# Pair units in 64-row tiles, even-odd tokens up to the store, low-rank products in row tiles, and totals carried by small transfers

## The chip, the cores and the metric

The kernel runs on one NeuronCore of a Trainium2 chip. The metric is device time in microseconds (us) of that core. Times and profiles come from the chip; in the profile PE is the matrix engine (TensorE), PEld its weight loads, DVE the VectorE, ACT the ScalarE, POOL the GpSimd engine, and SP the engine whose queue issues most of the transfers.

## The reference, cut to what matters

There are two stages. The first is a gated linear recurrence for 4 batches x 8 heads, 768 tokens, head size 48; the second adds a low-rank mix along the tokens and a two-layer MLP with a ReLU.

```
for t in range(S):                       # S = 768, state is D x D per head, D = 48
    state = alpha[:, :, t, :, None] * state + einsum('bhd,bhe->bhde', k[:, :, t], v[:, :, t])
    y[:, :, t] = einsum('bhd,bhde->bhe', q[:, :, t], state)
x = y as (batch, token, head * D)        # 4 x 768 x 384
h = x.transpose(0, 2, 1) @ U @ V         # U 768 x 32, V 32 x 768: mixes the tokens
u = x + h.transpose(0, 2, 1)
out = u + maximum(u @ w_ch1, 0) @ w_ch2  # 384 -> 1536 -> 384
```

## The kernel before

**Chunks.** The recurrence is computed in chunks of 128 tokens. Within a chunk the logarithms of alpha are summed up to each token by a matrix product with a triangle of ones; their exponentials scale q (upward) and k (downward); the scores, k times q, are masked to the lower triangle; the chunk's output is masked scores times v, plus q times the state that came into the chunk; and the state for the next chunk is (old state + scaled k times v), times the total decay of the chunk. Products run on TensorE in bf16 and land in PSUM[...]; DVE, ACT and GpSimd do the rest.

**Two layouts.** Batches 2 and 3 use `stage_gla`, one chunk of 128 tokens and all 8 heads a time: six units a batch. Batches 0 and 1 (`PAIR`) use `stage_pair`, which takes 256 tokens of 4 heads: partition p holds tokens 2p and 2p + 1 of the block (index j), so each descriptor of a load carries two tokens. A unit has two chunks (index c): the lower 64 partitions are chunk 0, the upper 64 chunk 1. The heads are taken in pairs (index a).

**Tokens in the pair units.** The transposed q (`qT`) is written by a copy with a stride (`f_ev` with swap), which puts a chunk's tokens in natural order. Scores (L486) run in 64 x 64 tiles of the array, four at a time. Outputs (L560 and L567) and state products (L518) run over all 128 rows: for that v lies in a wide buffer `rw` that has zeros where the other chunk would be, filled by two casts a unit (`f_rv`), so that one product of 96 or 192 columns serves both chunks, half of it on zeros.

**The mix.** `stage_mix` multiplies x by U for six chunks (L727): each product has 32 output rows, and the four column groups of the array (128 x 32 tiles) work side by side, each on other chunks, so that PSUM holds four partial sums on 128 partitions. V is there four times (`vm_sb`, made through `sel`), so that one product over all 128 rows adds them up: six products a batch (L758), and for batch 0 (`XT`) the same into the transposed layout (L749) and once more in the second MLP product (L836). After it come transposes (L774), the first MLP product (`mlp1`, L801, 72 matmuls a batch) and the second (`mlp2`, L831), with an add (L843) and a store (L848).

**Totals.** The decay of a chunk is needed per row of the state. In `stage_gla`, four products with one column of ones (L592) put the sums of a chunk across the partitions, and two exponentials (L605) with an offset of -30000 on the half that is not wanted make `tot` of them, by which `f_st` (L687) multiplies.

**What sets the order.** Each `P.add` records one step with the engines that it may run on, what it reads and writes, and, for TensorE, the shape of the array's tiles (F full, R 64 x 128, Q 64 x 64, C 128 x 32, V for 32 rows). The string `TABLE` lists the steps by number; a letter names the engine where a step has several (A for ACT, V for DVE, G for GpSimd). `Plan.run` emits them in exactly this order, so that TABLE sets each engine's order and, with it, SP's queue of loads and stores. `Plan.place` gives out buffers and PSUM banks along the way. In the first 28 us, products of zeros (`filler`, L317) are put in where the plan has gaps.

**Loads.** 24 loads of 192 KB a batch (alpha, k, q, v for six units) and 24 of the weights go into 36 buffers `io`; a load waits in SP's queue until its buffer is free. Batch 3 transposes q and k by a transfer from ACT's queue (L623) and not on TensorE.

Of the kernel before, what the change touches and what calls it, by code (L numbers as in the profile page):

```python
# [159 lines left out]
69 65 61 201 157 179 63 64 62 160 204 162 165V 73 66 67 71 77 159A 161 164G 158G 167 182 169V 184 163 206 183 207 224 205 75 166 173 70 168V 186V 174  # L160
187V 170 227 229 175 188 209V 189 68 191A 232G 228 247 171 211 190V 176 172 192 194 234 250 78 208G 230 213A 180A 251 236A 185 210 181G 212V 195 177 81
214 254G 193 178V 3 256 268 252 253 196 215 74 271 72 79 197 76 4 231G 82 83 80 273 199 233 203A 202G 235A 84 198 258V 216 217 255G 272 218 226G 219
274 225A 237 85 93 6 257 5 259A 222 220 240 25 29 27 89 15 17 13 19 23 21 87 33 94 35 86 31 238 239 200A 275G 223A 95 90 221 241 260 276V 242 277 249G
248G 279A 278 2 270G 243 245 261 263 244 262 47 92 280A 264 91 97 37 43 269A 281 265 284 39 41 51 49 101 88 45 285 266 96 0 1 8 30G 28G 283 282 286 388
246A 432 391 435 267V 287 298 18G 11 9 16G 14G 288V 394 7A 289 105 57 59 53 55 290 438 437 436 10A 12V 102 291A 100 103 20G 295 292 304 301 98 293 294V
24G 22G 307 296 299 302 308 297V 305 26A 410 99 306V 303V 413 300A 326 322 107 309A 350 336 416 393 392 337V 310 414 396G 334 324 325A 415 311V 327V
335V 351V 323V 34G 32G 104 106 109 108 110 344 342 320 340 346 338 318 321A 36A 343V 395V 319A 314 398 330 341A 345A 315A 339V 439V 417V 400V 440G 356
354 412G 117 111 357V 355V 397 352 441 328 331A 347A 443V 419 442 316 411A 418G 353V 329V 444V 420 332 455 399A 333A 317A 426 348 312 421V 422V 40A
349A 38G 44G 42G 427 458 313V 428 423 429G 390G 46G 401 445 460 459 461 48A 52A 425 446 424 402 368 358 363 433G 434G 389G 50A 478 430 481 482 483 484
54G 60G 58A 499 369 447 431V 403 373 359 404 364 448 405 406 407V 449 450V 485V 408 502 56A 503 456A 409V 486V 365 370 451 371 487 462G 463V 488 504  # L170
457A 507G 360 471 489A 490A 505 465 467A 464 361 366 479A 480A 113 367 119 118 466V 472 374 491 473G 506G 468 492 375 509 494 453 469 470 511A 112 508
474 452G 378 495 618 475G 620 476 510A 376 501A 496G 621 454V 512 493 500G 515 624G 379 514 497 516 517G 513 626 623 657 622 625V 477A 129 362 114 115
659 518 662 498A 519A 627 380 629A 520 521A 637 660 628V 630 381 632 383 661 663G 664G 619G 522 524 133 121 523 525 530 384 536 534 528 531 529 537 535
526 385 527A 532 116 120 124 125 127 141 123 122 134 533V 126 665 131 372 137 135 639 666 668V 633 538 539V 634 640 641 540 642 562 548 558 542 541A
563V 643G 644G 572 646 549V 559V 717 648V 631 667V 573A 645 544 582 556 677 647A 545A 557A 649 832 669 130 128 386 583V 671 566 568 670 651 650 554 719
546 584 567A 543A 721 720 555V 697 658A 585V 586 679 547V 587V 569V 578 681 722 638G 834 652 574 635 653 575V 836 835 680 636A 682 837 387 153 655 560
550 580 684V 656V 654V 552 699 683G 553V 551A 867 701 838G 704G 570 686 685 564 579V 581V 571V 565V 702 700 678A 561A 672 703V 687V 724V 593 588 706
705 692 594 595 673 598 589 675 145 132 674V 693 707V 596 708V 839V 676V 840 688A 849 709 689 711 710 691 690 723G 851 599 725 727A 576 698G 726 600
590 712 854 577A 869 841 728A 852 718A 591 694V 872 870 613 614 729 713 731 730 138 149 382 377 143 136 142 885 921 853 871 714G 147 139 615 603 887
715 732 695 601 716V 696V 604 842 733A 889 734 923 608 735A 855G 874G 616 844 843 738 748 873G 833G 744 903 888 925 924 926 742 609 749 743 745 602 592  # L180
140 146 155 154 750 751 739 892G 610 736 746 605 752 737 850G 890 875 876 747V 753V 740 845 847 905 846 794 796 741V 797V 606 856G 891G 927G 778 768
774 848A 857 611 795V 894 858 908 893 906 760 780 764 862 152 150 144 761V 148 151 612 156 617 775V 781V 765V 863 769V 788 782 800 790 798 784 791V
779V 785V 772 758 759V 789A 907 799A 773A 801A 754 755V 756 757V 877 859 895 860 861 878 896 904A 783A 776 762 928G 864G 807 770 766 929 930 868G 909G
886G 910G 763V 767V 771V 911 802 865 912 880 803 916 808 897 777V 881 882G 879 809 898 804 812 883 813 899 900V 810 805 931 913 917 932 884A 866A 914
933 915 918G 786 792 901 827 811 806 922G 793A 902A 787A 822 934 919 920A 823 824 935V 936 828 937A 829 938 940 946 825 939 947 941 817 814 944 826 597
607 945 818 942 948 949V 943A 950 819 820 951 956 966 968 952 830 953 815 962 974 954 960 975V 970 963V 955V 976 982 994 969V 961V 995V 971A 967V 1000
992 988 993A 977A 957A 978 986 964 987V 1001V 980 958 989V 981V 959A 984 1002 990 996 983A 965A 1003A 985V 991V 997A 998 999A 972 1014 1024 1015 1004
1025 1026 1019 1020 1027 979V 973V 1021 1005 1009 1010 831 816 1028 1022 1006 1016 1007 1011 1023 821 1008 1017 1029 1012 1030 1032 1018 1013 1031 1033
1034
# [3 lines left out]
def mm(*cols):  # L193
    return sum(max(c / 2.4 + 2.5, 25.0) for c in cols)
# [3 lines left out]
def kernel(  # L198
# [12 lines left out]
    nc = tc.nc  # L211
# [20 lines left out]
    TRD = {(3, c) for c in range(NC)}  # L232
# [5 lines left out]
    u_in = const.tile([128, NC, R], FP32, name="u_in")  # L238
    v_in = const.tile([R, S], FP32, name="v_in")
# [9 lines left out]
    mask2 = const.tile([C, 2, 2 * C], BF16, name="mask2")  # L249
    for x in (filler, tri, ident, mask2, blocks):  # L250
# [6 lines left out]
        out=mask2, in_=mask2, compare_op=ALU.is_gt, fill=1.0, base=0, pattern=[[1, 2], [-1, 2 * C]], channel_multiplier=2  # L257
# [26 lines left out]
    nc.vector.tensor_copy(maskp[0:64, 0], mask2[0:64, :, 0:C])  # L284
    nc.vector.tensor_copy(maskp[64:128, 0], mask2[64:128, :, C : 2 * C])
    rv2_s = slots("rw", 4, [C, 2, HP, 2, D], BF16)
    for x in rv2_s:
        nc.vector.memset(x, 0.0)
    maskc = const.tile([C, 1, C], BF16, name="maskc")
    P.add({"POOL": 250}, lambda e: nc.gpsimd.tensor_copy(maskc[:, 0, :], ut_ones), w=["maskc"])  # L290
    sel = const.tile([R, 4, R], BF16, name="sel")
# [8 lines left out]
    tots = Pool(slots("tot", 4, [128, HP * 2, 1], FP32))  # L300
    qts = Pool(slots("qt", 4, [128, HP, C], BF16))
# [31 lines left out]
    def small():  # L333
        P.add({"SP": 450.0}, lambda e: nc.sync.dma_start(u_in, moe_U.rearrange("(c p) r -> p c r", p=128)), w=["u_in"])
        P.add({"SP": 500.0}, lambda e: nc.sync.dma_start(v_in, moe_V), w=["v_in"])
        P.add({"POOL": 300, "ACT": 280}, lambda e: copy(e, u_sb, u_in), r=["u_in"], w=["u"])
        P.add({"POOL": 800}, lambda e: nc.gpsimd.tensor_copy(v_bf, v_in), r=["v_in"], w=["v_bf"])
        for i in range(2):
            vb = Buf(bank)
            sl = slice(i * TW, (i + 1) * TW)  # L340
            P.add({"PE": mm(TW)}, lambda e, vb=vb, sl=sl: nc.tensor.matmul(vb()[:, 0:TW], lhsT=sel.rearrange("r a b -> r (a b)"), rhs=v_bf[:, sl], start=True, stop=True), r=["v_bf"] + [("sel", g) for g in range(4)], w=[vb], mode="V")
            P.add({"DVE": 470, "ACT": 390}, lambda e, vb=vb, sl=sl: copy(e, vm_sb[:, sl], vb()[:, 0:TW]), r=[vb], w=[("vm", i)])

    def weight(dst, src, key, engs):
        t = Buf(io)
        P.add({"SP": 590.0}, lambda e: nc.sync.dma_start(flat(t), src), w=[t])
        P.add(engs, lambda e: copy(e, dst, flat(t)), r=[t], w=[key])
# [4 lines left out]
    def weights1():  # L352
        for g in range(4):
            cs = slice(g * DM, (g + 1) * DM)
            for ct in range(NCT):
                weight(w1_sb[:, ct, cs], moe_w_ch1[ct * 128 : (ct + 1) * 128, cs], ("w1", g, ct), {"POOL": 485, "ACT": 435})

    def weights2():
        for jt in range(NJ):
            weight(w2_sb[:, jt, :], moe_w_ch2[jt * 128 : (jt + 1) * 128, :], ("w2", jt), {"POOL": 485, "ACT": 435})  # L360
# [24 lines left out]
    def xk(b, xb, c):  # L385
        return [(xb, c, 0), (xb, c, 1)] if b in PAIR else [(xb, c)]

    def stage_pair(b, u, sprev, xb):
# [12 lines left out]
        rv = Buf(rv2s)  # L401
# [5 lines left out]
        for c in range(2):  # L407
            P.add({"POOL": 480, "ACT": 420}, lambda e, c=c: f_rv(e, c), r=[vt], w=[(rv, c)])
# [494 lines left out]
```

## Time and profile before

| what | before |
|---|---|
| three runs: median (lowest to highest) | 164.61 us (163.31 to 165.84) |
| the profiled execution, in all | 164.47 us |
| its span, first to last instruction | 162.7 us |
| PE busy, share of the span | 154.3 us, 95% |
| DVE | 125.8 us, 77% |
| ACT | 85.4 us, 52% |
| POOL | 57.7 us, 35% |
| granted TensorE clock | 0.998 |
| HBM read, written | 23.79 MB, 4.72 MB |

A row of the groups gives line, engine, operation, what is written and read, shape and count; then the busy time and the mean of one; then the engine's idle time just before, and what ended it. Matmuls overlap in the array, so their mean is longer than the step from one to the next; the steps come from the starts. A row of the chain of waits has the start, the length and the work. A row of stretches has, for each, its bounds and length, the busy time of the five engines with counts, the clock, the DMA share and GB/s.

### The profile page before, as it was taken

Reading aid. Unit: us, or ns where it says so; the run is one execution under the profiler, and the core shown is the slowest. Engines: PE = TensorE matmul, PEld = TensorE weight load, DVE = VectorE, ACT = ScalarE, POOL = GpSimd, SP = SyncE. Lnnn points to the kernel's source line nnn. Section 1 sums busy time; section 2 is a strip of 40 time slices with the busy share of each in tenths; the row PEclk is TensorE's granted clock in tenths of the full one; section 3 lists DMA queues with packets and bytes.
Section 4 is the critical chain, followed back from the end, with each engine's and each line's share of the span. In section 5 each row is a group of like instructions: output and inputs, shape, how many; then the busy total and the mean of one; then the engine's idle time right before and its main releaser. Section 6 shows DMA issues by size and latency. Waiting matters only on the chain.

```text
span 162.7 us, 4458 instructions
## 1 busy us (share of the span) xinstructions
PE 154.3 (95%) x1683; PEld 102.4 (63%) x1683; DVE 125.8 (77%) x274; ACT 85.4 (52%) x218; POOL 57.7 (35%) x92
## 2 busy tenths in 40 slices
PE   7789999999999899999999999999899999999993
PEld 2356787667776676766666666766466656666662
DVE  6478996689969996979999888988978557961441
ACT  5479899557885778468982386307102411153000
POOL 3037985756264172550092056634413000000000
PEclk9999999999999999999999999999999999999999
DMA  5999999999999998998997898989982040200134
GB/s 124 271 279 302 250 277 285 326 316 330 355 253 248 207 209 185 186 202 168 216 246 64 198 204 209 218 135 189 218 108 99 0 144 7 97 0 4 48 145 145
DMA packets 89701, 30.37 MB, mean 187 GB/s; under 512 B 83376, under 2 KB 89648, under 8 KB 89680
## 3 DMA queue, kind: packets, MB, share of 16 engines
q1 hardware_dynamic: 83152, 28.52, 71.1%
q10 hardware_dynamic: 6528, 1.57, 7.4%
q8 instruction: 13, 0.21, 0.6%
q14 instruction: 8, 0.07, 0.1%
HBM read 23.79 MB, written 4.72 MB: 175 GB/s over the span
## 4 chain that ended last, share of the span: by engine, by line
PE 84%; DVE 6%; ACT 3%; DMA 3%; issue 1%; SPq 1%; DVEq 0%; ACTq 0%
PE ps L801 29%; PE ps L831 27%; PE ps L459 3%; DMA io<-in_alpha_dram 3%; PE ps L653 2%; PE ps L567 2%; PE ps L774 2%; DVE rq L446 2%; PE ps L486 2%; PE ps L758 2%; PE ps L632 2%; PE ps L518 1%; PE ps L712 1%; PE ps L590 1%; DVE st L531 1%
## 5 line engine op out<-in xcount | busy, mean ns | idle before, releaser
L831 PE MATMUL ps<-w_sb,h1t 128*128 128x384 bf16 (+2 forms) x300 | 53.1, 319 | 0.0
L801 PE MATMUL ps<-uT,w_sb 128*128 128x384 bf16 x288 | 50.9, 326 | 0.0
L801 PEld LDWEIGHTS <-w_sb 128*128 128x128 bf16 x288 | 26.8, 98 | 16.2 <-DVE uT L326 0.2
L831 PEld LDWEIGHTS <-h1t 128*128 128x128 bf16 x300 | 27.2, 98 | 15.2 <-issue 0.3
L813 DVE TENSOR_SCALAR h1t<-ps 128x384 bf16<-128x384 f32 x59 | 30.0, 551 | 6.4 <-PE ps L801 6.3
L811 ACT ACTIVATE h1t<-ps 128x384 bf16<-128x384 f32 x37 | 16.8, 500 | 16.7 <-PE ps L801 16.5
L843 DVE TENSOR_TENSOR ou<-ub,ps 128x384 f32<-128x384 bf16 (+2 forms) x19 | 9.9, 529 | 10.5 <-PE ps L831 10.3
L612 POOL TENSOR_TENSOR rk<-io,ai 128x384 bf16<-128x384 f32 x11 | 10.7, 977 | 16.7 <-ACT ai L600 11.2
L497 DVE TENSOR_TENSOR pm<-ps,maskp 128x512 bf16<-128x512 f32 x24 | 15.7, 684 | 0.3 <-PE ps L486 0.2
L663 DVE TENSOR_TENSOR pm<-ps,maskc 128x512 bf16<-128x512 f32 x24 | 15.2, 684 | 0.7 <-PE ps L653 0.6
L324 ACT CAST xb<-ps 128x384 bf16<-128x384 f32 x13 | 5.9, 480 | 14.2 <-PE ps L712 14.2
L759 DVE TENSOR_TENSOR ub<-xb,ps 128x384 bf16<-128x384 bf16 x18 | 9.0, 550 | 2.5 <-PE ps L758 2.5
L687 POOL TENSOR_TENSOR st<-sm,tot 128x384 bf16<-128x384 f32 x4 | 3.3, 828 | 18.6 <-DVE sm L699 18.6
L328 POOL CAST w_sb<-io 128x384 bf16<-128x384 f32 x16 | 7.9, 505 | 5.4 <-DMA io<-in_moe_w_ch_dram 5.2
L446 POOL TENSOR_TENSOR rk<-io,ai 128x384 bf16<-128x384 f32 x7 | 6.4, 912 | 9.1 <-ACT ai L431 6.3
L324 ACT COPY qt<-ps 128x512 bf16<-128x512 bf16 x11 | 7.7, 700 | 3.2 <-PE ps L459 1.9
L612 POOL TENSOR_TENSOR rq<-io,aa 128x384 bf16<-128x384 f32 x8 | 7.3, 914 | 2.7 <-issue 1.6
L400 ACT ACTIVATE lt<-io 128x384 bf16<-128x384 f32 x12 | 6.3, 530 | 2.9 <-DMA io<-in_alpha_dram 2.9
L317 PE MATMUL ps<-filler 128*128 128x512 bf16 x17 | 6.5, 510 | 1.2 <-DVE filler L251 1.2
L326 DVE CAST xb<-ps 128x384 bf16<-128x384 f32 x11 | 6.1, 554 | 1.8 <-PE ps L712 1.5
L446 POOL TENSOR_TENSOR rq<-io,aa 128x384 bf16<-128x384 f32 x6 | 5.9, 981 | 4.2 <-ACT aa L432 3.9
L605 ACT ACTIVATE tot<-ps,offb 128x4 f32<-128x4 f32 x24 | 4.9, 274 | 4.7 <-PE ps L801 4.5
(124 smaller groups left out, 266.2 us busy)
## 6 DMA issues: line engine op xcount, KB each, us to landing
io<-in_alpha_dram SPq DMA_DIRECT2D x24, 192.0 KB, 4.1
io<-in_q_dram SPq DMA_DIRECT2D x24, 192.0 KB, 4.3
io<-in_v_dram SPq DMA_DIRECT2D x24, 192.0 KB, 4.1
io<-in_k_dram SPq DMA_DIRECT2D x24, 192.0 KB, 4.2
io<-in_moe_w_ch_dram SPq DMA_DIRECT2D x24, 192.0 KB, 4.4
out_dram<-ou SPq DMA_DIRECT2D x23, 192.0 KB, 2.3
out_dram<-ou SPq DMA_DIRECT2D x1, 128.0 KB, 1.7
v_in<-in_moe_V_dram SPq DMA_DIRECT2D x1, 96.0 KB, 3.5
```

What stands on the lines that cost most here:

```text
L324: nc.scalar.copy(dst, src)
L328: nc.gpsimd.tensor_copy(dst, src)
L446: eng.tensor_tensor(jh(dst()[:, :, 0:D]), raw(a), jh(x()), op=ALU.mult)
L497: nc.vector.tensor_tensor(dst, s2, maskp.to_broadcast([C, 2, 2, C]), op=ALU.mult)
L612: eng.tensor_tensor(dst()[:, :, 0:D], a(), x(), op=ALU.mult)
L663: nc.vector.tensor_tensor(pm()[:, :, par, :], s2, maskc.to_broadcast([C, HP, C]), op=ALU.mult)
L759: P.add({"DVE": 465}, lambda e, c=c, hb=hb: nc.vector.tensor_tensor(ub()[:, c, :], xb()[:, c, :], hb()[:, 0:DM], op=ALU.add), r=[hb] + xk( ...
L801: nc.tensor.matmul(hb()[:, 0:TW], lhsT=w1_sb[:, ct, jt * 128 : (jt + 1) * 128], rhs=uT()[:, ct, tt * TW : (tt + 1) * TW], start=(ct == 0), ...
L811: nc.scalar.activation(dst, hb()[:, 0:TW], AF.Relu)
L813: nc.vector.tensor_scalar_max(dst, hb()[:, 0:TW], 0.0)
L831: nc.tensor.matmul(hb()[:, 0 : hi - lo], lhsT=h1()[:, jt, c * C : (c + 1) * C], rhs=w2_sb[:, jt, lo:hi], start=(jt == 0), stop=(jt == NJ - ...
L843: nc.vector.tensor_tensor(ou()[:, lo:hi], base()[:, c, lo:hi], hb()[:, 0 : hi - lo], op=ALU.add)
```

## The change

It has six parts.

1. **Pair units in 64-row tiles** (`HALF`, batches 0 and 1). v is cast once into a plain buffer. State products are made for each chunk on its own 64 rows (tile shape R), into a bank each, and so are the outputs from the masked scores (`f_yn`); the part from the state (`f_yi`) follows over full rows. The output copy is made for each chunk.
2. **Even-odd tokens.** Within a chunk, the even tokens come first and then the odd ones, up to the store. The transposes write q in that order (`swap` is now in the product's output pattern), the copy is a plain one, and the mask is built for it. U and V are kept in both orders (`up_sb`, `vp_sb` for batches 0 and 1); U is brought back to natural order by a product with a permutation, V by a copy on GpSimd. The store writes every second row of the output from each half.
3. **Low-rank products in row tiles** (`ROWS`, batches 1 to 3). The product with U uses two sums instead of four, each made twice (12 products a batch instead of 6), so that 64 rows hold all of x times U. Then two chunks are multiplied by V at once, one on each half of the rows.
4. **Totals by transfers** (`TOTD`, batches 2 and 3). The four products and two exponentials go. One exponential (`f_end`) is taken over the last 32 rows of the sums, and two small transfers on SP's queue carry its last row to the 48 partitions of either half of a `tot` that is zero elsewhere. The halves of `tot` are now stored one after the other.
5. **Casts on DVE.** Casts of v and of weights may run on DVE too.
6. **A new TABLE**: the whole order is another one, with other choices of engines (it is not shown: 30 lines of numbers).

The diff, cut to its core:

```diff
-    TRD = {(3, c) for c in range(NC)}
+    HALF = (0, 1)
+    ROWS = (1, 2, 3)
+    TOTD = (2, 3)
+    TRD = {(3, c): "kq" for c in range(NC)}
...
-    rv2_s = slots("rw", 4, [C, 2, HP, 2, D], BF16)
-    for x in rv2_s:
+    totz_s = slots("totz", 4, [128, HP * 2, 1], FP32)
+    rv2_s = slots("rw", 4 if len(HALF) < len(PAIR) else 0, [C, 2, HP, 2, D], BF16)
+    for x in totz_s + rv2_s:
         nc.vector.memset(x, 0.0)
...
+            lambda e: nc.tensor.matmul(
+                ub_()[:, 0 : NC * R], lhsT=perm, rhs=up_sb.rearrange("p c r -> p (c r)"), start=True, stop=True
+            ),
...
-        for c in range(2):
-            P.add({"POOL": 480, "ACT": 420}, lambda e, c=c: f_rv(e, c), r=[vt], w=[(rv, c)])
+        if apart:
+            P.add({"POOL": 480, "ACT": 420, "DVE": 340}, lambda e: copy(e, flat(rv), flat(vt)), r=[vt], w=[(rv, 0), (rv, 1)], port=True)
...
-            d = d.rearrange("x (a m j) -> x a j m", a=2, j=2) if swap else d.rearrange("x (a j m) -> x a j m", a=2, j=2)
-            copy(e, d, t)
+        def f_ev(e, dst, tb):
+            copy(e, dst().rearrange("x e c -> x (e c)"), bf(tb())[:, 0:512])
...
+                if apart:
+                    for c in range(nch):
+                        r = slice(64 * c, 64 * c + 64)
+                        for m in parts:
+                            nc.tensor.matmul(
+                                db[c]()[m, a * 2 * D : (a + 1) * 2 * D],
+                                lhsT=rk()[r, HP * j + 2 * a : HP * j + 2 * a + 2, :].rearrange("t h w -> t (h w)")[:, m],
+                                rhs=raw(rv)[r, j, 2 * a : 2 * a + 2, :],
+                                start=(n == 0), stop=(n == 3 and not onpe), skip_group_check=True,
+                            )
+                    continue
...
+        if apart:
+            yb = [Buf(bank) for _ in range(2)]
+            def f_yn(e):
+                for h in range(HP):
+                    for j in range(2):
+                        for c in range(2):
+                            r = slice(64 * c, 64 * c + 64)
+                            for m in parts:
+                                nc.tensor.matmul(
+                                    yb[c]()[m, h * D : (h + 1) * D], lhsT=pm()[r, (h // 2) * 2 + j, h % 2, m], rhs=raw(rv)[r, j, h, :],
...
+            for c in range(2):
+                P.add(
+                    {"ACT": 225, "DVE": 260},
+                    lambda e, c=c: copy(e, xb()[:, 2 * blk + c, half * Q : (half + 1) * Q], yb[c]()[:, 0:Q]),
...
+        moved = b in TOTD
+        sums = c < NC - 1 and not moved
...
+        def f_end(e):
+            nc.scalar.activation(end()[C - 32 : C].rearrange("t i d p -> t p i d"), cb()[C - 32 : C, 0:DM].rearrange("t (p i d) -> t p i d", i=2, d=D), AF.Exp)
+
+        def f_move(e, i):
+            nc.sync.dma_start(tot()[64 * i : 64 * i + D, HP * i : HP * i + HP, 0], end()[C - 1 : C, i].rearrange("t d p -> t (d p)"))
...
-                nc.tensor.matmul(
-                    xu()[32 * g : 32 * g + R, 0:DM], lhsT=u_sb[:, c, :], rhs=xb()[:, c, :],
-                    start=(c < 4), stop=(c + 4 >= NC), skip_group_check=True,
-                )
+                for gg in (g % 2, g % 2 + 2) if twice else (g,):
+                    nc.tensor.matmul(
+                        xu()[32 * gg : 32 * gg + R, 0:DM], lhsT=us[:, c, :], rhs=xb()[:, c, :],
+                        start=(c < (2 if twice else 4)), stop=(c + (2 if twice else 4) >= NC), skip_group_check=True,
+                    )
...
+        def f_low(e, c):
+            for i in range(2):
+                r = slice(64 * i, 64 * i + 64)
+                nc.tensor.matmul(hbs[c + i]()[:, 0:DM], lhsT=vs[r, (c + i) * C : (c + i + 1) * C], rhs=utx()[r], start=True, stop=True)
...
+                rows = out[b, c * C : (c + 1) * C, lo:hi]
+                if b in PAIR:
+                    rows = rows.rearrange("(m j) x -> j m x", j=2)
+                nc.sync.dma_start(rows, ou()[:, lo:hi])
```

## The prediction

> **What bounds the kernel now.** I read the busy line first, then the sums over two stretches, the chain of waits in one short window, the two places where the weight loads stood still, and the matmul groups by shape.
>
> ```profile
> PE 154.3 (95%) x1683; PEld 102.4 (63%) x1683; DVE 125.8 (77%) x274; ACT 85.4 (52%) x218; POOL 57.7 (35%) x92
> ```
>
> ```profile
> core 0: us, PE busy (x) PEld busy (x) DVE busy (x) ACT busy (x) POOL busy (x), PEclk, DMA share, GB/s
> 0.00:29.00 29.00, 25.20 (x363) 17.08 (x364) 21.91 (x70) 22.96 (x57) 15.46 (x33) 1.00 0.96 257
> 29.00:160.00 131.00, 129.08 (x1324) 85.36 (x1320) 103.68 (x205) 62.43 (x162) 42.23 (x60) 1.00 0.77 173
> ```
>
> TensorE is the bound, but in one of two stages. From 29.05 us, where the first MLP product (L801) starts, to 159.9 us it has work all the time. Before, batch 0's attention runs as its inputs land, and the chain hops between ACT, DVE and PE. From the last matmul to the end are 2.8 us (an add and a store).
>
> ```profile
> 63.96 0.43 PE ps L727 x6
> 64.39 0.33 PE ps L653 x8
> 64.72 0.76 PE ps L831 x4
> 65.48 0.49 PE ps L758 x3
> 65.97 0.65 PE ps L831 x4
> ```
>
> This window gives the prices. L831 normally takes 0.65 us for four: 0.162 a matmul of 384 columns, columns at 2.4 GHz and little else. L653's eight products of 128 columns use 64-row tiles in pairs: four pairs of 0.056 are 0.22, yet 0.33 are shown; and the four L831 after them take 0.76, not 0.65. So each change of tile shape, either way, costs about 0.1 us. The starts of single matmuls give 258 against 162 ns on the way in and 148 against 56 on the way out: **0.095 us a change**. Full matmuls of 96 columns (L567) follow each other every 42 ns, of 48 columns (L712) every 25, of one column (L592) every 25. With these prices the dense stretch is 127.9 us of pure stream and some 3 us of stall, of which two pieces make 2.0:
>
> ```profile
> 53.47 0.23 PEld L459 LDWEIGHTS <-rq 128*128 128x128 bf16 x4 [1.08 <-DVE rq L446]
> ...
> 115.77 0.23 PEld L653 LDWEIGHTS <-kt 48*128 48x128 bf16 x8 [0.96 <-DMA kt<-rk]
> ```
>
> The groups that the change rewrites (their mean is the time through the array, not the step between two):
>
> ```profile
> L567 PE MATMUL ps<-rw,pm 128*128 128x96 bf16 x96 | 6.0, 206 | 0.0
> ...
> L758 PE MATMUL ps<-utx,vm_sb 128*128 128x384 bf16 x18 | 4.4, 326 | 0.0
> ...
> L518 PE MATMUL ps<-rw,rk 128*128 128x192 bf16 x32 | 4.0, 246 | 0.4 <-ACT rw L324 0.4
> ...
> L592 PE MATMUL ps<-ones,lt 128*128 128x1 bf16 x48 | 2.9, 164 | 0.0
> ...
> L727 PE MATMUL ps<-xb,u_sb 128*32 128x384 bf16 x24 | 2.0, 333 | 0.0
> ```
>
> **What the Trainium skill says.** "TensorEngine Tiling (Array Packing)", Key Properties: changing the tiling mode drains TensorE. The trace agrees, with 0.095 us. The same page, Gotcha 1 (PSUM Pressure): row tiles must write different banks; the new code does so and takes two banks where it took one. "TensorE: Matmul & The Clock Gate", the section on 56 against 53.3 ns: start to start never falls under about 25 ns. The trace agrees for full tiles (L712, L592). "DMA: Bandwidth & Descriptors", Anatomy of one DMA: a fixed cost near 2 us, told there for GpSimd's path; the nearest row here, on SP's, the 64 KB store, landed in 1.6.
>
> **The change on TensorE.** Counts are from the two instruction orders.
> - State updates of the pair units (L518): 32 of 192 columns (0.0825) and 16 of 96 become 32 pairs and 16 single ones of 96 columns: 32 x (0.0825 - 0.0425) = 1.28 saved, half of it in batch 0.
> - Their outputs (L567): 96 x 0.0425 become 96 pairs of 48 columns. No row shows such a pair. If the floor holds per tile it takes 0.025, if per instruction 0.050. L653's pairs start 3 ns apart and L486's four tiles share 0.056, 14 ns a matmul, so instructions can follow faster than 25 ns; I take 2 x 14 = 0.028: 1.39 saved, half in batch 0. Ends: 1.68 saved, 0.72 lost.
> - Totals of batches 2 and 3 (L592): 48 x 0.025 = 1.20 saved, all dense.
> - Low-rank products (L758): 18 x 0.1625 become 9 pairs: 1.46 saved. The product with U ahead of them needs three waves of 0.1625 instead of two in three batches: 0.49 lost. U's permutation adds 0.08.
> - Tile-shape changes: 39 become 70; after the first MLP product 24 become 41, 17 x 0.095 = 1.62 lost.
> Dense: 0.64 + 0.70 + 1.20 + 1.46 - 0.49 - 0.08 - 1.62 = 1.81 saved. One cumulative sum of batch 1 (0.43) now stands after the first MLP product, not before: **1.4 us** left.
>
> **The change elsewhere.** qT's swapped copy (0.73 on DVE, 0.70 on ACT) becomes a plain one as kT's (0.42, 0.58). V is cast once a unit, not twice: 12 casts of 0.5 fewer, mostly on GpSimd. Four memsets (1.5 us of DVE) go. An xb copy splits into two (0.35 estimated each on DVE, from the 192-column state row): some 0.15 more for each. Eight ReLUs go from DVE to ACT. DVE gets about 7 us lighter, ACT 2 heavier: neither was the bound in the dense stretch (104 and 62 of 131). In batch 0 DVE is busy nearly throughout from 7.8 to 26.8 us; its work there falls by about 0.6 us, ACT's by 1.9, and the landing of inputs doesn't move: the last V is again the 24th load. I take **0.6 us** off the opening, from 0 to 1.5.
>
> Twenty small transfers of totals join SP's queue, between the loads of batches 2 and 3. Each waits there for an exponential on ACT, and the loads queued behind it wait too; the state update on DVE or GpSimd waits for its landing. They stand ahead of that update by several instructions, so I cost them at nothing; cover is the MLP of the batch before. The even-odd store writes the same 1536-byte rows: nothing. V's and U's reordering runs on GpSimd, idle 65%: nothing.
>
> Stalls: the 1.08 came from DVE with its rq late; DVE is lighter, I count it gone. The 0.96 of the transposing transfer stays. New: between the U product and the paired low-rank product stand only four MLP matmuls (0.65 + 0.1), while the copy between them took until 0.71 after the first: 0.1 for each of three. Stalls **0.8 us** less; bounds +1 and -2.3.
>
> Sum: 162.7 - 1.4 - 0.6 - 0.8 = 159.9 us span; the profiled execution took 164.47 in all, 1.77 around the span: 161.7. It lies 0.14 below the median of the runs shown: **161.8 us**, 1.7% less.
>
> **The rivals.** (1) The new order also closes the second stall and the opening tightens: stalls to 0.8 us, opening -1.2: 162.7 - 1.4 - 2.3 - 1.2 + 1.8 = 159.6. For it: DVE, the last cause in most waits, is lighter. Against: a transposing transfer caused the second stall, and these stay.
> (2) Row pairs don't overlap below 25 ns an instruction: dense outputs 48 x 0.022 and updates 16 x 0.0075 dearer, 1.2 together, opening and stalls unmoved: 164.4, no change. Against: L486's 14 ns.
> (3) Slower: the totals block SP's queue. It is in use or waiting nearly throughout from 57 to 115 us, at 0.36 to 0.7 us an issue; 20 more are 7 to 14 us. Batch 3's last V was issued at 114.5 and cast at 125.9, so it has 11 us; beyond that each microsecond delays batch 3's outputs, and after them only some 5 us of other MLP work is left. At 0.7 and with waits for ACT behind, 3 to 5 us late: about 168. It decides once an issue with its wait costs over 0.55 us. Against: gaps of 4 to 5 us in the queue that are waits for other transfers, and totals that need only alpha.
>
> **How the numbers follow.** Forecast 0.50, (1) 0.23, (2) 0.15, (3) 0.12. 2% of the median is 3.3 us (161.3 and 167.9), about what a measurement of this kernel can tell from no change. The forecast's own range is 160.4 to 163.6, and some 0.15 of its chance lies under 161.3; so faster is 0.38, slower 0.10, same 0.52. The range leaves out most of (3) and the outer half of (1): 159.4 to 165.4.
>
> **What would show it.** A step of 25 to 30 ns for pairs in the new output lines (L617), against 50; 41 changes at 0.095 in the dense stretch; the first MLP product (L953) near 28.4 us; its stalls near 2.3 us; no SP wait for the exponentials of the totals (L705) that a PE wait follows. I would be wrong if the opening grew, if PSUM banks, used faster now, made TensorE wait for evictions, or if loads of batch 3 came late.

## The result, and the profile after

The changed kernel takes **194.25 us** (192.21 to 195.22 in four runs) against 163.96 (163.02 to 165.84 in four): 1.178 times as long, with a 95% interval of 1.162 to 1.194. The forecast was 161.8, and the range ended at 165.4. Its profiled execution took 192.21 us, with a span of 190.4. Ratios here and below leave disturbed executions out, so that the quotient of two medians can differ from them a little.

Busy time, granted clock and the shares of the chain of waits, from the page of the changed kernel:

```profile
PE 163.7 (86%) x1783; PEld 102.3 (54%) x1783; DVE 118.3 (62%) x272; ACT 91.7 (48%) x215; POOL 55.1 (29%) x87
...
PEclk9999999999999999999999955996999759999999
...
PE 43%; DMA 25%; SPq 14%; DVE 6%; issue 5%; ACT 4%; POOL 1%; ACTq 1%; DVEq 0%; POOLq 0%
```

The last of these lines, before:

```profile
PE 84%; DVE 6%; ACT 3%; DMA 3%; issue 1%; SPq 1%; DVEq 0%; ACTq 0%
```

TensorE made 84% of the chain before; it makes 43% now, and transfers with SP's queue make 39%. DVE, ACT and GpSimd are idle more than they were. No engine has become the bound: the kernel waits. The stretches of the changed kernel say where (bounds and length, then busy time of PE, PEld, DVE, ACT, POOL with counts, clock, DMA share, GB/s):

```profile
core 0: us, PE busy (x) PEld busy (x) DVE busy (x) ACT busy (x) POOL busy (x), PEclk, DMA share, GB/s
0.00:29.00 29.00, 25.70 (x424) 16.54 (x425) 20.33 (x72) 21.21 (x58) 13.05 (x28) 1.00 0.93 251
29.00:187.00 158.00, 137.63 (x1358) 85.51 (x1356) 97.44 (x200) 70.49 (x159) 42.02 (x59) 0.94 0.67 144
...
60.00:80.00 20.00, 18.01 (x218) 11.58 (x212) 14.83 (x32) 13.89 (x30) 6.01 (x9) 1.00 0.64 129
80.00:100.00 20.00, 16.99 (x191) 11.33 (x189) 15.63 (x30) 10.15 (x21) 6.18 (x8) 1.00 0.70 129
100.00:120.00 20.00, 11.68 (x88) 6.09 (x88) 6.82 (x15) 6.47 (x13) 2.46 (x3) 0.74 0.59 122
120.00:140.00 20.00, 16.90 (x131) 9.96 (x129) 14.17 (x29) 6.51 (x13) 6.37 (x9) 0.91 1.15 144
140.00:160.00 20.00, 16.43 (x159) 9.53 (x156) 10.66 (x21) 4.19 (x9) 2.27 (x4) 0.83 0.39 98
```

The same stretches of the kernel before, as far as its loads of batch 3 go:

```profile
60.00:80.00 20.00, 20.00 (x233) 13.49 (x230) 17.58 (x35) 14.82 (x40) 6.05 (x9) 1.00 0.93 192
80.00:100.00 20.00, 19.89 (x246) 13.42 (x245) 18.09 (x36) 11.67 (x35) 8.65 (x10) 1.00 0.99 181
100.00:120.00 20.00, 19.21 (x181) 12.37 (x179) 17.55 (x36) 6.59 (x20) 8.98 (x12) 1.00 1.02 185
```

The opening is what it was. From 60 us on, when the first stores and the loads of batches 2 and 3 share the transfer engines, the core moves 122 to 129 GB/s instead of 181 to 192. The last of the 96 input loads is issued at 143.8 us; before it was at 114.5. And in the stretch from 100 us TensorE makes 88 matmuls instead of 181.

The span grew by 27.7 us. The starts of the matmuls divide it. The dense stretch is the time from the first MLP product to the last matmul; its stream is the count of matmuls of each shape, times the prediction's step durations (26.6 ns for the new pairs of 48 columns), plus 0.095 us a change of tile shape; what is left is stall. The parts: first MLP product at 28.36 instead of 28.92 (-0.6), dense stream 126.36 instead of 127.67 (-1.3), **stalls in the dense stretch 32.4 instead of 3.1 (+29.3)**, tail +0.3. Some 5 us of these stalls are matmuls at half the step rate: about 30 steps of 384 columns took 0.32 us instead of 0.16, in the slices where the granted clock is 5 to 7 tenths. They stand in three stretches (from 109, 129 and 151 us), and gaps of TensorE of 2.2 to 2.5 us stand ahead of each. A gap of 3.0 us at 87 us has no such stretch behind it, so the length of one gap doesn't decide. The kernel before has no such steps, and neither has `e1_two_stores` below; I take them for a consequence of the waits.

What TensorE waited for, in the chain of the changed kernel from 96 to 132 us (start, length, work):

```profile
101.35 10.81 DMA out_dram<-ou
...
112.19 0.04 DVE ou L995
...
116.16 10.88 DMA out_dram<-ou
...
127.13 0.55 DVE ou L995
127.69 0.94 DVE h1t L965 x2
...
128.67 2.28 PE ps L953 x9
```

These two stores take 10.8 and 10.9 us from issue to landing, each right behind another even-odd store; six others up to 130 us take 6.9 to 7.4 by their semaphores. The add L995, which needs the store's buffer, comes after it, then two ReLUs (L965), then the MLP product (L953). The waits of the page say the same for the whole span (engine, what waited, for what: us in total, times, longest):

```profile
POOL rk L722 <- DMA io<-in_k_dram: 19.5, 3, 10.4
DVE ou L995 <- DMA out_dram<-ou: 19.2, 5, 7.3
POOL rv L342 <- DMA io<-in_v_dram: 16.5, 2, 10.8
ACT lt L676 <- DMA io<-in_alpha_dram: 14.0, 3, 7.0
```

DVE stands for 19.2 us until an output buffer is free, and what is queued behind these adds (ReLUs, masks, copies) stands with it. GpSimd and ACT stand for inputs. How much of the loss goes through the buffers and how much through late inputs was not separated. Before the change, the longest wait for a transfer in this view was 5.2 us in all (GpSimd, for weights).

The packet records of the trace show why a store is slow. Up to 130 us, where all stores are even-odd ones, never more than 34 packets of 1536 bytes start within one microsecond while they run, at 65 ns each: 34 x 0.065 = 2.2 engines busy with them. Before, up to 250 start within one (several stores at once), at the same 65 ns: 16 engines. So the 128 rows of one store need 128 x 0.065 / 2 = 4.2 us on two engines, besides what else is queued there, and twelve such stores hold these two for 50 us. The Trainium skill states the rule: "DMA: Bandwidth & Descriptors", the section on why a DMA increments its semaphore by 16 and not by 1, says that the number of engines is the largest one up to 16 that divides the slowest dimension of both access patterns. The pattern `(m j) x -> j m x` puts j, of size 2, outermost. The trace agrees: two engines, and the count of semaphore updates goes the same way: an even-odd store leaves 3 in the trace, any other store 16. The page's median landing of a store (2.3 us before, 2.0 in the changed kernel) says nothing of this, for it leaves out every even-odd store.

Totals by transfers show in two rows of the groups and issues (ACT's exponential for them, and the transfers' size and median landing):

```profile
L705 ACT ACTIVATE end<-ps 32x384 f32<-32x384 f32 x10 | 8.4, 858 | 1.5 <-DMA totz<-end 1.3
...
totz<-end SPq DMA_DIRECT2D x20, 0.8 KB, 3.6
```

The exponential takes 0.86 us; the two that it replaces took 0.54 together. A small transfer lands 3.6 us after its issue.

### The profile page after: what moved, and what is told of

Its sections match the earlier page's. It is cut to its first block, busy times and chain, and to the rows that moved or that the text cites. A ratio compares the mean times of both kernels' runs of the same rounds, so it can differ in the third digit from the quotient of the medians.

```text
span 190.4 us, 4669 instructions
## 1 busy us (share of the span) xinstructions
PE 163.7 (86%) x1783; PEld 102.3 (54%) x1783; DVE 118.3 (62%) x272; ACT 91.7 (48%) x215; POOL 55.1 (29%) x87
## 4 chain that ended last, share of the span: by engine, by line
PE 43%; DMA 25%; SPq 14%; DVE 6%; issue 5%; ACT 4%; POOL 1%; ACTq 1%; DVEq 0%; POOLq 0%
PE ps L983 17%; PE ps L953 16%; DMA out_dram<-ou 15%; SPq L411 8%; DMA io<-in_v_dram 5%; DMA io<-in_moe_w_ch_dram 2%; DMA kt<-rk 2%; DVE pm L769 2%; SPq L418 2%; PE ps L507 1%; SPq L387 1%; ACT end L705 1%; SPq L708 1%; DVE ub L911 1%; DVE ou L995 1%
## 5 line engine op out<-in xcount | busy, mean ns | idle before, releaser
L983 PE MATMUL ps<-w_sb,h1t 128*128 128x384 bf16 (+2 forms) x300 | 58.1, 338 | 2.5 <-DVE ou L995 2.5
L953 PE MATMUL ps<-uT,w_sb 128*128 128x384 bf16 x288 | 52.2, 332 | 2.2 <-ACT h1t L963 2.0
L983 PEld LDWEIGHTS <-h1t 128*128 128x128 bf16 x300 | 28.1, 102 | 21.5 <-issue 8.2
L953 PEld LDWEIGHTS <-w_sb 128*128 128x128 bf16 x288 | 27.6, 99 | 19.5 <-issue 3.7
L965 DVE TENSOR_SCALAR h1t<-ps 128x384 bf16<-128x384 f32 x51 | 25.8, 551 | 11.2 <-PE ps L953 11.0
L995 DVE TENSOR_TENSOR ou<-ub,ps 128x384 f32<-128x384 bf16 (+2 forms) x19 | 9.9, 532 | 32.5 <-DMA out_dram<-ou 19.2
L963 ACT ACTIVATE h1t<-ps 128x384 bf16<-128x384 f32 x45 | 20.7, 498 | 17.3 <-PE ps L953 10.3
L676 ACT ACTIVATE lt<-io 128x384 bf16<-128x384 f32 x12 | 6.2, 524 | 22.8 <-DMA io<-in_alpha_dram 14.0
L342 POOL CAST rv<-io 128x384 bf16<-128x384 f32 x12 | 6.0, 502 | 16.7 <-DMA io<-in_v_dram 16.5
L492 POOL TENSOR_TENSOR rq<-io,aa 128x384 bf16<-128x384 f32 x8 | 7.8, 985 | 9.1 <-ACT lt L441 5.7
L338 ACT CAST xb<-ps 128x192 bf16<-128x192 f32 (+1 forms) x19 | 7.0, 381 | 6.7 <-PE ps L851 2.5
L722 POOL TENSOR_TENSOR rq<-io,aa 128x384 bf16<-128x384 f32 x8 | 7.2, 913 | 7.5 <-ACT aa L696 5.6
L338 ACT CAST rv<-io 128x384 bf16<-128x384 f32 x9 | 4.6, 535 | 9.7 <-DMA io<-in_v_dram 9.7
L705 ACT ACTIVATE end<-ps 32x384 f32<-32x384 f32 x10 | 8.4, 858 | 1.5 <-DMA totz<-end 1.3
L696 ACT ACTIVATE aa<-ps 128x384 bf16<-128x384 f32 x12 | 5.7, 497 | 6.3 <-DMA qt<-rq 4.5
L342 POOL CAST w_sb<-io 128x384 bf16<-128x384 f32 x12 | 5.8, 506 | 7.4 <-DMA io<-in_moe_w_ch_dram 7.4
```

What stands on the lines that cost most here:

```text
L338: nc.scalar.copy(dst, src)
L342: nc.gpsimd.tensor_copy(dst, src)
L492: eng.tensor_tensor(jh(dst()[:, :, 0:D]), raw(a), jh(x()), op=ALU.mult)
L722: eng.tensor_tensor(dst()[:, :, 0:D], a(), x(), op=ALU.mult)
L953: nc.tensor.matmul(hb()[:, 0:TW], lhsT=w1_sb[:, ct, jt * 128 : (jt + 1) * 128], rhs=uT()[:, ct, tt * TW : (tt + 1) * TW], start=(ct == 0), ...
L963: nc.scalar.activation(dst, hb()[:, 0:TW], AF.Relu)
```

## The experiments

Each ratio is against the kernel before on the same chip; "gap" is the ratio less one, times that kernel's median, in us. `e10_dummy_transfers`, `e11_store_halves_act` and `e12_even_odd_b0` ran on another chip than the rest, on which the kernel before has a median of 162.81 us and not 163.3 to 163.4; so ratios are compared, and not times. Stalls and loads come from one profiled execution a kernel, and executions of the kernel before alone differ by some 2 us. The theory ahead of these runs was that the store's outermost dimension is the cause of nearly all of it; the rivals were the totals in SP's queue (the prediction's own third rival) and the new order or the 64-row tiles themselves.

| run | ratio (95%) | gap | stalls in the dense stretch | last load issued |
|---|---|---|---|---|
| kernel before, as profiled | 1 | 0 | 3.1 | 114.5 |
| changed kernel | 1.178 (1.162 to 1.194) | 29.2 | 32.4 | 143.8 |
| `e1_two_stores` | 1.022 (1.018 to 1.027) | 3.6 | 7.2 | 124.9 |
| `e2_before_two_way` | 1.140 (1.132 to 1.148) | 22.8 | 24.5 | 132.2 |
| `e3_plain_rows` | 1.014 (1.007 to 1.021) | 2.3 | 4.4 | 121.7 |
| `e4_four_way`, a single run | 175.83 us against 163.34 | 12.5 | 15.0 | 130.7 |
| `e5_totals_on_pe` | 1.003 (1.000 to 1.005) | 0.4 | 3.1 | 117.8 |
| `e7_natural_totals_pe` | 1.002 (0.998 to 1.005) | 0.2 | 2.8 | 115.4 |
| `e8_end_contiguous` | 1.026 (1.019 to 1.033) | 4.2 | 8.1 | 126.8 |
| `e9_totals_act_queue` | 1.012 (1.005 to 1.019) | 2.0 | 5.6 | 121.9 |
| `e10_dummy_transfers` | 1.025 (1.019 to 1.031) | 4.0 | 6.6 | 126.8 |
| `e11_store_halves_act` | 1.013 (1.009 to 1.018) | 2.1 | 4.2 | 116.4 |
| `e12_even_odd_b0` | 1.005 (1.002 to 1.008) | 0.8 | (5.0) | (118.9) |

### The store: four runs

**One part undone.** The changed kernel, with each even-odd store issued as two transfers of 64 rows, so that the rows come outermost:

```diff
-                    rows = rows.rearrange("(m j) x -> j m x", j=2)
-                nc.sync.dma_start(rows, ou()[:, lo:hi])
+                    for j in range(2):
+                        nc.sync.dma_start(rows.rearrange("(m j) x -> j m x", j=2)[j], ou()[64 * j : 64 * j + 64, lo:hi])
+                else:
+                    nc.sync.dma_start(rows, ou()[:, lo:hi])
```

> The changed kernel, with each even-odd store of batches 0 and 1 given as two transfers of 64 rows in place of one whose outermost dimension is 2. Theory A (the store in one piece runs on two of the 16 DMA engines: 32 packets of 1536 bytes a microsecond at 65 ns each, so 4.2 us a store, with loads, output buffers and later stores behind it): the packets come at over 100 a microsecond, the waits of DVE for out_dram go, and the time falls to 159 to 164 us. Theory B (the 20 small transfers of totals hold SP's queue and make the loads late): the stores are not the cause, the time stays over 185 us. If both have a part, it lands between, at 165 to 180.

Measured: 166.9 us, ratio 1.022, above theory A's range and in the lower end of "both have a part". Of the 29.2 us, 25.6 are gone with the same bytes, the same rows and twelve issues more. Its group of adds and their wait for output buffers, and the group of the kernel before:

```profile
L995 DVE TENSOR_TENSOR ou<-ub,ps 128x384 f32<-128x384 bf16 (+2 forms) x19 | 9.8, 530 | 14.5 <-PE ps L983 10.9
...
DVE ou L995 <- DMA out_dram<-ou: 3.3, 3, 2.2
...
L843 DVE TENSOR_TENSOR ou<-ub,ps 128x384 f32<-128x384 bf16 (+2 forms) x19 | 9.9, 529 | 10.5 <-PE ps L831 10.3
```

The wait for output buffers falls from 19.2 to 3.3 us; the adds wait mainly for TensorE, as they did before.

**One part done alone.** The kernel before, where only the store of batches 0 and 1 gets the new pattern:

```diff
-                lambda e, lo=lo, hi=hi: nc.sync.dma_start(out[b, c * C : (c + 1) * C, lo:hi], ou()[:, lo:hi]),
+                lambda e, lo=lo, hi=hi: nc.sync.dma_start(
+                    out[b, c * C : (c + 1) * C, lo:hi].rearrange("(m j) x -> j m x", j=2) if b in PAIR else out[b, c * C : (c + 1) * C, lo:hi], ou()[:, lo:hi]
+                ),
```

> The kernel before, with the store pattern of the changed kernel alone (outermost dimension 2) in batches 0 and 1; the rows of these batches so land in other places of the output. Theory A: 12 stores of 128 packets at 65 ns on two engines, 4.2 us each, in a stretch in which the DMA share is near 1.0: 175 to 195 us. Theory B: no totals by transfer here, 163 to 166 us.

Measured: 186.54 us, ratio 1.140: 22.8 us from the store alone. Its group of adds, and that of the changed kernel:

```profile
L843 DVE TENSOR_TENSOR ou<-ub,ps 128x384 f32<-128x384 bf16 (+2 forms) x19 | 10.1, 532 | 29.6 <-DMA out_dram<-ou 19.8
...
L995 DVE TENSOR_TENSOR ou<-ub,ps 128x384 f32<-128x384 bf16 (+2 forms) x19 | 9.9, 532 | 32.5 <-DMA out_dram<-ou 19.2
```

The adds wait 19.8 us for output buffers, as long as those of the changed kernel do (19.2). Nothing else of the change is in this kernel.

**The dose.** Four ways instead of two, in the changed kernel:

```diff
-                    rows = rows.rearrange("(m j) x -> j m x", j=2)
+                    rows = rows.rearrange("(m j) x -> j m x", j=4)
```

> The changed kernel with an outermost dimension of 4 in the stores of batches 0 and 1; the rows of these batches so land in other places. Theory A, if the outermost dimension sets how many engines take part: 64 packets of 1536 bytes a microsecond, 2.1 us a store, and a time between, 164 to 174 us. If the cause is the stride of the rows in memory and not the number of engines: as the changed kernel, 32 packets and over 185 us. Theory B: over 185 us.

Measured: 175.83 us in a single run, a little above theory A's range. Up to 125 us, never more than 68 packets of 1536 bytes start within one microsecond (4.4 engines busy), and such a store leaves 5 semaphore updates. Two engines 194, four 176, all of them 167: twice the engines take the store's share of the gap from 25.6 to 8.9 us (12.5 less the 3.6 that is not the store's).

**Without the reordering at the store.** The rearrangement is left out, and the store is one of 128 rows in a row:

```diff
-                if b in PAIR:
-                    rows = rows.rearrange("(m j) x -> j m x", j=2)
```

> The changed kernel with contiguous stores everywhere, one transfer each; the rows of batches 0 and 1 so stay in even-odd order in the output. Theory A: as the two-transfer form or up to 1 us faster, for it has 12 issues fewer on SP: 159 to 164 us. Theory B: over 185 us.

Measured: 165.7 us, ratio 1.014, above the range. The twelve issues that the two-transfer form adds, and its stride of two rows, cost about the 1.3 us between this and `e1_two_stores`; the two intervals overlap a little, so that this isn't certain.

What follows: with the store as it stood, the store's pattern is about 26 of the 29 us (22.8 measured on the kernel before, 25.6 on the changed one). Some 3.6 us are left to explain.

### The totals: four runs

**Totals back on TensorE.** As `e1_two_stores`, and the column products and the two exponentials are back in batches 2 and 3; `TABLE` stays, and the two small transfers of a chunk become empty steps in it.

```diff
-            for p in range(HP if sums else 0):
+            summed = c < NC - 1
...
+            for p in range(HP if summed else 0):
...
-            P.add({"ACT": 400}, f_end, r=[cb], w=[end])
+            P.add({"ACT": 400}, f_tot, r=[cb, (tot, 0), (tot, 1)], w=[end])
...
-                P.add({"SP": 120}, lambda e, z=z: f_move(e, z), r=[end], w=[(tot, z)])
+                P.add({"SP": 120}, lambda e: None, r=[end], w=[(tot, z)])
```

> The changed kernel with two-transfer stores, and with the totals of batches 2 and 3 made on TensorE and ACT as before (40 products of one column, 20 small exponentials; the 20 transfers are gone). It is to be read against the two-transfer form with 166.9 us. Theory C (the rest of the loss comes from the totals: their issues and waits in SP's queue, and their exponential at 0.86 us on ACT where 0.40 was planned, make loads and steps of batches 2 and 3 late): 1.0 us of stream is added, the stalls after 80 us fall from 5.9 to under 3, and the time is 163.5 to 165.5 us. Theory D (the rest comes from the order and the 12 more store issues, not from the totals): 166.9 + 1.0, 167 to 168.5 us.

Measured: 164.24 us, ratio 1.003, in theory C's range, where `e1_two_stores` has 1.022. So the transfers cost 3.2 us, although they save TensorE 1.0 us of stream (127.36 with the products, 126.36 without). The chain of waits of `e1_two_stores` from 100 to 130 us:

```profile
110.42 5.20 DMA kt<-rk
...
115.63 3.52 DMA io<-in_q_dram
...
119.61 3.40 DMA kt<-rk
...
123.02 3.16 DMA io<-in_v_dram
...
126.77 0.33 PE ps L782 x4
```

and that of this run in the same window:

```profile
108.02 4.18 DMA kt<-rk
...
112.20 0.52 ACT lt L676
...
113.08 2.44 PE ps L954 x15
```

With the transfers, the time is set almost throughout by loads and by transposing transfers, one after the other, until 126.8 us; without them TensorE sets it from 113.1 on. In the queue of SP, in `e1_two_stores`, one sees what stands ahead of the last loads (start, length in the queue with its wait, line):

```profile
113.10 1.70 SPq L708 DMA_DIRECT2D totz<-end  x1
...
117.38 0.96 SPq L708 DMA_DIRECT2D totz<-end  x1
...
119.02 2.09 SPq L708 DMA_DIRECT2D totz<-end  x3
...
123.02 0.37 SPq L418 DMA_DIRECT2D io<-in_v_dram  x1
...
124.86 0.59 SPq L418 DMA_DIRECT2D io<-in_v_dram  x1
```

All twenty take 16.1 us of the queue, 0.81 each with their waits, and the last load is issued at 124.9 us instead of 117.8.

**Which part of them?** Three causes are possible: the place in the queue, the state update's wait for the landing, and ACT's long exponential. The first alone: `e5_totals_on_pe`, with the 20 small transfers at their places in SP's queue, to a tile that nothing reads.

```diff
+                P.add({"SP": 120}, lambda e, z=z: nc.sync.dma_start(aside[c % 4][64 * z : 64 * z + D, HP * z : HP * z + HP], end()[C - 1 : C, z].rearrange("t d p -> t (d p)")), r=[end], w=[(tot, z)])
```

> The form with two-transfer stores and totals on TensorE (164.2 us), with the 20 small transfers put back in SP's queue at the same places and after the same steps, but to a tile that nobody reads; ACT writes four elements for them in some 0.2 us. If the transfers harm by their place in the queue (issue, waits, the loads behind them): the last load is issued at 121 to 125 us instead of 117.8 and the time is 165.5 to 167. If the harm is in the wait of the state update for their landing or in the exponential of 0.86 us: 164 to 165 us.

Measured: 167.61 us, ratio 1.025: by the gaps 3.6 us more than `e5_totals_on_pe`, as much as the totals cost, within the intervals. The last load is issued at 126.8 us, later than expected. In the chain of waits, the block of 15 MLP products that started at 113.08 above now comes after a later load of k:

```profile
108.85 4.50 DMA io<-in_k_dram
...
116.65 2.44 PE ps L962 x15
```

Nothing waits for these transfers but the next use of their source; a small exponential of four elements (0.17 us) goes along with each pair. The run doesn't part the issues from their waits for ACT. They took 13 us of the queue, 0.65 each, less than those of `e1_two_stores`, so that the loss isn't simply in step with that time. The transfers' own packets, of 4 and 16 bytes, are busy for under 1 us on sixteen engines in all (`e1_two_stores`), too little to be a rival.

The exponential alone: its output written in reading order instead of at a stride of 16 bytes.

```diff
-            nc.scalar.activation(end()[C - 32 : C].rearrange("t i d p -> t p i d"), cb()[C - 32 : C, 0:DM].rearrange("t (p i d) -> t p i d", i=2, d=D), AF.Exp)
+            nc.scalar.activation(end()[C - 32 : C].rearrange("t i d p -> t (i d p)"), cb()[C - 32 : C, 0:DM], AF.Exp)
```

> The two-transfer form with the exponential of the totals writing its result in the order in which it reads it, not transposed to a step of 16 bytes; the totals so reach wrong rows and the output is another. Measures the strided write: mean of L705 from 0.86 to 0.45 us or less. Theory C, if the exponential's length on ACT is what hurts: 165 to 166 us; if the transfers themselves are: 166.4 to 167.2. Theory D: 166.4 to 167.2.

The rows of this exponential, its durations as minimum, median and maximum in ns:

```profile
L705 ACT ACTIVATE end<-ps x10: 467/483/485, 60.6 to 119.7; 32x384 f32<-32x384 f32 x10
```

0.48 us instead of 0.86, and the kernel takes 167.97 us, not less than `e1_two_stores` (1.026 against 1.022, with intervals that overlap). It is above both ranges. The long exponential isn't it.

Another queue: `nc.sync` becomes `nc.scalar` in `f_move`.

> The two-transfer form with the 20 transfers of totals issued from ACT's queue and not SP's. Theory C, if SP's queue is the place of the harm: loads of batches 2 and 3 are issued earlier and the time falls to 164.5 to 166; ACT pays some 0.1 us an issue. Theory C, if the landing or the exponential is the place: 166 to 168. Theory D: 166.5 to 168.

Measured: 165.72 us, ratio 1.012. About half of the 3.2 us goes, and the last load is issued at 121.9 us, still later than the 117.8 without the transfers. An issue took 0.56 us of ACT's queue (median of the twenty), not the 0.1 of the expectation, and one state update on GpSimd waited 6.5 us for a landing. Which of the two makes up the other half was not separated.

### What is left: three runs

**The even-odd order undone as well.** As `e5_totals_on_pe`, with natural order in batches 0 and 1: plain stores, the swapped copy of qT, and U, V and the mask as before. 64-row tiles, row-tiled low-rank products and the new order stay.

```diff
-                moe_U.rearrange("(c m j) r -> j m c r", c=NC, j=2)[j]
+                moe_U.rearrange("(c j m) r -> j m c r", c=NC, j=2)[j]
...
-                if b in PAIR:
-                    rows = rows.rearrange("(m j) x -> j m x", j=2)
```

> The changed kernel with its even-odd part undone (natural order of tokens, the swapped copy of qT, one contiguous transfer a store) and with the totals on TensorE; what stays is the 64-row tiles, the low-rank products in row tiles, and the order. Theory C: the swapped copies cost 12 x 0.2 to 0.3 us of DVE and ACT, partly on the path in the opening, and the 12 issues are saved: 162.5 to 165. Theory D, with the order to blame: 165 to 167.5.

Measured: 163.77 us, ratio 1.002 (0.998 to 1.005), so this can't be told from the kernel before, nor from `e5_totals_on_pe`, from which it is 0.2 us away with intervals of 0.4 and 0.6 us to either side. With the store in two transfers neither a cost nor a gain of the even-odd order is seen.

**The halves on two queues.** `e5_totals_on_pe`, with the second half of each even-odd store issued from ACT's queue:

```diff
+                        (nc.scalar if j else nc.sync).dma_start(rows.rearrange("(m j) x -> j m x", j=2)[j], ou()[64 * j : 64 * j + 64, lo:hi])
```

> The form with two-transfer stores and totals on TensorE, the second half of each such store issued from ACT's queue: 12 issues fewer on SP. If the 12 issues are what keeps the loads late (last at 117.8 against 114.5 before): 163 to 164 us, below the kernel before by 0 to 0.5. If not, or if ACT, waiting for the add, holds up its own steps: 164.2 to 166.

Measured: 164.96 us, ratio 1.013: the gain didn't come. The last load is indeed issued a little earlier (116.4 instead of 117.8), and the kernel is 1% longer than with both halves on SP. The twelve issues cost ACT's queue 0.5 us each; what relieving SP's queue alone would earn isn't shown by this.

**The even-odd order in batch 0 alone**, where it was to shorten the opening, and natural order in batch 1 (one step of `TABLE`, V's copy on GpSimd, is moved ahead):

```diff
+    EVEN = (0,)
...
-                if b in PAIR:
-                    rows = rows.rearrange("(m j) x -> j m x", j=2)
-                nc.sync.dma_start(rows, ou()[:, lo:hi])
+                if b in EVEN:
+                    for j in range(2):
+                        nc.sync.dma_start(rows.rearrange("(m j) x -> j m x", j=2)[j], ou()[64 * j : 64 * j + 64, lo:hi])
+                else:
+                    nc.sync.dma_start(rows, ou()[:, lo:hi])
```

> Two-transfer stores and totals on TensorE, with the even-odd order in batch 0 alone; batch 1 keeps natural order, with the swapped copy of qT. Batch 0's attention is where DVE and ACT set the pace: the first MLP product should start at 28.3 us as in the even-odd form, against 29.2 in the natural one, and 6 of the 12 extra issues go. If the opening is worth its 0.9 us: 162.8 to 163.8. If the stalls after it take the place of the gain: 164 to 165.

Measured: 163.74 us, ratio 1.005 (1.002 to 1.008). The time lies in the range of a gain, but only because the kernel before is shorter on this chip as well; the ratio says 0.8 us longer. The first MLP product is at 28.30 us, as hoped. The profiled execution took 165.55 us, 1.8 above the median, so that its stalls and its last load (in brackets in the table) don't explain the median. No version beat the kernel before.

## Why the prediction was wrong

**The step that failed: "The even-odd store writes the same 1536-byte rows: nothing."** It looked at the length of a row and not at the order of the dimensions. What the pattern changes is how many engines share the transfer: 2 instead of 16, so 4.2 us a store at least, some 7 with the other traffic on them, and 10.8 behind another such store. That is 22.8 us on the kernel before and 25.6 between the changed kernel and its two-transfer form. The page that states the rule is cited in the prediction for the fixed cost of a transfer alone; its section on the number of engines, which bears on this edit, was left aside, and no rival had it either. A bound from both sides shows what was at stake: 12 stores x 128 rows x 0.065 us is 100 engine-microseconds, which is 6 us on sixteen engines and 50 on two.

**The second step that failed: the totals' transfers "at nothing".** They cost 3.2 us. The cover named there, that the transfers stand ahead of the state update, is not the one that counts: with nobody reading them they cost 3.6. What the runs point to is the place in SP's queue, with loads behind them, which was the prediction's third rival. Its price of 3 to 5 us fits, its place fits (batch 3's loads), and its point of decision fits: an issue with its wait costs 0.81 us, over 0.55. It was given a chance of 0.12, and its 168 us is near the 166.9 of the kernel with the store mended.

**Dense stream: 1.4 us less forecast, 1.3 by the counts in the trace.** Of the prices in it, those of the pairs and of the change of shape were measured anew. The row of the changed kernel that answers to L567, and those for L518 and L758:

```profile
L617 PE MATMUL ps<-rv,pm 64*128 64x48 bf16 x192 | 4.3, 181 | 0.3 <-DVE pm L542 0.3
...
L570 PE MATMUL ps<-rv,rk 64*128 64x96 bf16 x80 | 4.1, 205 | 0.0
...
L903 PE MATMUL ps<-utx,vm_sb 64*128 64x384 bf16 x12 | 2.0, 418 | 2.9 <-DVE utx L340 2.2 <-DVE ou L995 0.7
```

From the starts, L617's pairs of 48 columns follow each other every 26.6 ns (28 forecast), so rival 2 falls. The changes of tile shape are 70 (29 before the first MLP product, 41 after), and one costs 0.095 us again: 258 against 162 ns on the way in, and about as much on the way out of L617 (111 ns, where steps inside it take 3 to 23).

**Opening: 0.6 us less forecast, and not shown.** The profiles have 28.36 after and 28.92 before, by the start of the same product. Yet `e2_before_two_way`, which up to its first store (54 us) is the kernel before, has 28.32. Seven of the nine runs with even-odd order in batch 0 have 28.1 to 28.6 us; `e8_end_contiguous` and `e4_four_way`, which change nothing there, have 29.1 and 29.3, and `e7_natural_totals_pe` with natural order has 29.24. Executions of one order so differ by as much as the forecast gain.

**Stalls: 0.8 us less forecast.** They are 29.3 more, from the two steps above. Even with store and totals out of the way they stay at 3.1 (`e5_totals_on_pe`) and 2.8 (`e7_natural_totals_pe`), where the forecast had 2.3. Of the 2.8 us that the forecast hoped for, the profile of `e5_totals_on_pe` has 0.3 us less of stream (it keeps 1.0 for the totals' products) and 0.7 less of opening, with the scatter just told, yet 20 executions of it aren't shorter than the kernel before. Its one profiled execution has a span of 162.0 us against 162.7, less than executions of one kernel differ by. Which wait takes the rest back isn't settled. That the 64-row tiles or the row-tiled low-rank products were worth anything by themselves wasn't tried: neither was undone alone.

**What would make it wrong** named late loads of batch 3 and full queues; that sign appeared. A wait for output buffers was not named.

## What to carry to other kernels

When a diff reorders a transfer's access pattern, look at the size of its outermost dimension as well as at the length of its rows: a 2 there left two of sixteen engines, and two transfers with the rows outermost gave the time back. A small transfer in a queue that feeds a late stage is priced by what is queued behind it: twenty of 0.8 KB that nobody read, with their small exponentials, cost 3.6 us. Before a part is priced at nothing because its bytes are the same, work out what it would take on one engine, and ask which view of the profile excludes that.

## What the runs showed that was not expected

- A slow store is felt through the add: DVE stands at the add, and with it the ReLUs behind it that feed TensorE. So 50 us of two engines' time, spread over two batches, became 23 to 26 us of the kernel.
- Behind gaps of 2.2 to 2.5 us TensorE's steps of 384 columns took 0.32 us instead of 0.16 for a while, some 5 of the 29 us; behind one of 3.0 us they didn't.
- An exponential over 32 x 384 values from PSUM takes 0.86 us when it writes at a stride of 16 bytes and 0.48 when it writes in a row.
- Two issues of half a store from two queues were not better than two from one (1.013 against 1.003).
